# Mamba-2 scan and maxout FFN in one kernel: another order of the first transfers, and the transposes of chunk 2 one step later

## The chip, the cores and the metric

The kernel runs on one core of a Trainium2 chip. The metric is the time of one execution on the device, in microseconds (us); lower is better. A core has a matrix engine (PE, with its weight loads PEld), a vector engine (DVE), a scalar engine (ACT), a general engine (POOL) and a queue engine that issues the transfers (SP, "SPq" in the profile). Each works through its own instructions in the order in which they were written; semaphores tie the engines together. All large transfers of this kernel are issued by SP and go through one queue that feeds sixteen DMA engines.

## The reference

The input is `x` (4 batches, 8 heads, 768 tokens, 32 values), a decay `a` per token, and `B` and `C` (16 values per token and head). Per head it is a gated recurrence over the tokens, here written in pieces of 32 tokens:

```
cum = cumsum(log a)                       # inside the piece
L   = exp(cum_i - cum_j), for j <= i      # decay between two tokens
y   = ((C B^T) * L) x  +  (C state) * exp(cum_i)
state = exp(sum log a) * state + B^T (x * exp(cum_last - cum_j))
```

The eight heads of a token, side by side, are a row of 256 values. All 3072 rows then go through a feed-forward block with a maximum of three products:

```
h   = max(x @ w1, x @ w2, x @ w3)         # 256 -> 768
out = h @ w_out                           # 768 -> 256
```

The activations are float32. The four weight matrices arrive as float64 and are turned into float32 on the chip.

## The kernel before

**Tiling.** The kernel cuts the 768 tokens into six chunks (0 to 5) of 128 tokens, and each chunk of all four batches is a block of 512 rows. For each chunk it computes the scan first, which leaves `yT` (256 x 512), and then the feed-forward block. The decay between tokens needs, for each chunk c, a tile `L` of 128 x 4 x 8 x 128 values: the running sums of log a are stored once to DRAM (`cums`, L713), and each chunk's are loaded back, spread over 128 partitions, in two halves of 1 MB (`decay_load`, L365; pair 0 is batches 0 and 1, pair 2 is batches 2 and 3). `last_load` (L373) loads the same sums in another layout as `E`, in eight small transfers; `load` (L125) loads `B`, `C` and `x` of a chunk. `fetch` (L159) loads one of twelve pieces of the weights, 512 KB each, nine of w1 to w3 and three of w_out. All of these stand in SP's one queue in the order of the program.

**Decoding the weights.** `decode` takes the next fetched piece through ACT (L175, L184), DVE (L176, L179) and POOL (L185); `sign` (L188, DVE) finishes it. This is done once, while chunk 0 is in its feed-forward block.

**The scan of a chunk n.** `transposed(n)` puts `B` and `C` through PE (L403, four transposes each, into `trB` and `trC`), copies `trB` to `BT` on ACT (L399) and, on POOL, makes `Bd` (L434). `scan_c` makes `CT` from `trC` on ACT (L418), `scan_e` is an exponential of `E` on ACT (L422), `scan_cd` multiplies `trC` and `E` on DVE (L429). `decay_masks(n, (b, b'))` masks two batches of `L` on POOL (L377), and `decay_part` takes the exponential of four heads of one batch on ACT (L384). `scores` makes the score products on PE (L474) and leaves their weighting on DVE (L482) for later. `scan_state` is the product for the next state on PE (L444, into a bank called `A`); it returns the rest, `scan_sum`, which is one multiplication on DVE (L455) and two operations on POOL (L460, L463). `scan_old`, `scan_own` make y on PE (L497, L510), `scan_y` copies it to `yT` on ACT (L534), `scan_sums` queues four differences on DVE (L544).

**The feed-forward block.** Chunk 0 is computed by plain products in a loop over n = 0 to 17 (L569), with the decoding and the scan of chunk 1 written between them. Chunks 1 to 5 are computed with seven products of half the size instead of eight, over nine steps k = 0 to 8 (three pairs of columns of each of the three matrices). In a step, `early` issues four products on PE (L619), a copy on ACT (L644) and three additions on DVE (L645 to L647); `late` issues the other three products, which go into the same two PSUM tiles (`sumA` of which there is one, `sumB` of which there are two), and then an operation that empties `sumA` (L658 on ACT, or L660 on DVE) and one that empties `sumB` (L661). The products need sums of weights that POOL makes, four operations for a step (`weight_sums`, L604 to L607); those for steps 2 to 8 are made in chunk 1's block, two steps ahead. `down_next` is a third of a quarter of the product with w_out (L681).

**What sets the order.** The order is written out by hand. While chunk c is in its feed-forward block, the scan of chunk n = c + 1 is written between `early` and `late` of its steps. For c = 1 the tables X1, Y1, P1, D1 and K1 (L855 to L860) say what stands at each step: in X1, "t" is `transposed(n)`, "s0" and "s2" are scores, "A" and "A1" the state product of chunk n and of chunk 1, "y" the end of the scan, "D" a `down_next`. P1 says how many of the operations kept for later (`later`) are taken from the list at three points of a step. The place between chunk 0's last product and chunk 1's step 0 (L842 to L850) is called the seam below.

Of the kernel before, what the change touches and what calls it, by code (L numbers as in the profile page):

```python
# [19 lines left out]
def kernel(  # L20
# [22 lines left out]
    NB, NH, S, D = x.shape  # L43
# [164 lines left out]
    load(0, "C")  # L208
    fetch()
    load(0, "x")  # L210
    for _ in range(4):
        fetch()


    ident = const.tile([P, P], FP32, name="ident")
# [409 lines left out]
    def pop(n):  # L625
        while n and later:
            later.pop(0)()
            n -= 1
# [63 lines left out]
    for b in range(2, NB):  # L692
# [19 lines left out]
    running(R, lg, a_sb)  # L712
    nc.sync.dma_start(  # L713
        out=cums.rearrange("k c s -> (k c) s").rearrange("(w r) s -> r w s", w=2), in_=a_sb)
    decay_load(1, (0,))
    fetch()
    decay_load(1, (2,))
    fetch()
    load(1, "B")
    load(1, "C")  # L720
    fetch()
    last_load(1)
    fetch()
    load(1, "x")
    fetch()
    decode()
    first_exps(2, True, (1,))
    first_exps(3, True, (1,))
# [54 lines left out]
    for n in range(NF * 3):  # L783
        j, g = divmod(n, 2)
        q, i = divmod(j, 3)
        f = 2 * q + g
        if n == 0:
            pair = [ffn_bank([P, BLK], "up") for _ in range(2)]
            for p, ff in zip(pair, range(2)):
                group(p, 0, ff, (0,))  # L790
            first_own((2, 3))
            for p, ff in zip(pair, range(2)):
                group(p, 0, ff, (1,))
        if j > 0:
            p = ffn_bank([P, BLK], "up")
            whole_group(p, i, f)
        else:
            p = pair[g]
        if i == 0 and g == 0:
            m = ffn.tile([P, 4, HB], FP32, tag="m", name="m")  # L800
        if n in (13, 14, 16, 17):
            pop(2)
        mg = m[:, 2 * g:2 * g + 2].rearrange("p r t -> p (r t)")
        if i == 0:
            nc.scalar.copy(out=mg, in_=p)
        else:
            nc.vector.tensor_tensor(
                out=mg if i == 1 else h_of(0)[:, f], in0=mg, in1=p, op=ALU.max)
        if g == 0 and n <= 16:
            sign()  # L810
            if n <= 14:
                decode()
        if n == 1:
            fj = from_last(R, a_sb, "fj")
        if n == 2:
            fetch()
            fetch()
            loads(2)
        if n == 3:
            first_tokens()  # L820
            scan_state(0, att_bank)()
        if n == 4:
            decay_masks(1, (0, 1))
        if n == 9:
            decay_masks(1, (2, 3))
        if n in (5, 7, 9, 11, 13, 14, 15, 16):
            part(1)
        if n == 10:
            transposed(1)
            scan_c(1)  # L830
# [14 lines left out]
    scan_own(1, range(NB))  # L845
    scan_y(1)
    scan_sums(1)
    pop(9)
    transposed(2)
    downs += [(0, j) for j in range(8)]  # L850

    X1 = ["A1", "", "D", "s0", "D", "s2", "A", "y", "D"]  # L855
    Y1 = ["", "", "D", "", "", "D", "D", "D", "D"]
    P1 = [(1, 1, 1), (1, 0, 0), (1, 0, 0), (1, 4, 1), (1, 0, 0), (1, 2, 2), (1, 1, 0), (1, 0, 0),
          (9, 0, 0)]
    D1 = [(1, 0), (1, 0), (2, 0), (1, 0), (2, 0), (1, 0), (0, 2), (0, 1), (0, 2)]
    K1 = {0: (0, (2, 3)), 4: (1, (0, 1)), 6: (1, (2, 3))}  # L860
# [8 lines left out]
    for c in range(1, NC):  # L869
# [4 lines left out]
        for k in range(NW):  # L874
# [79 lines left out]
```

## Time and profile before

| what | value |
|---|---|
| median of 3 runs | 311.21 us (310.51 to 312.63) |
| the profiled execution | 310.39 us, its span 308.7 us |
| mean granted clock of TensorE | 0.983 |
| busy: PE | 284.7 us, 92% of the span |
| busy: DVE, ACT, POOL | 198.6, 120.8 and 72.4 us |
| DMA queue of SP | 104688 packets, 27.66 MB, 44.4% of the 16 engines' span |

All times of the trace count from the start of the span. A row of the timeline names start, length, engine, line, operation, output and inputs, and how many instructions are put together in it; in square brackets stands how long the engine was idle before it and what ended that. A float32 product is shown as two records. A row of a table of windows gives, for one stretch of time, the busy time of each engine, the granted clock of TensorE (1.00 is full speed) and the mean busy share of the DMA engines. A "DMA" piece in the chain of waits reaches from the issue of a transfer to its landing.

### The profile page before, as it was taken

The numbers are of one execution on the slowest core, as the hardware profiler recorded it, in microseconds if no ns is written. First come the engines' busy times: TensorE is split into PE (matmuls) and PEld (weight loads), VectorE is DVE, ScalarE is ACT, GpSimd is POOL, SyncE is SP. The second block draws the span as 40 slices with busy tenths as digits, with TensorE's granted clock in tenths as the row PEclk, the third lists the DMA queues.
The fourth block names the chain that finished last, engine by engine and source line by source line (L and its number), as shares of the span: only waits on it lengthen the run. The fifth ranks groups of instructions, "written<-read, shape, count | busy, mean of one in ns | idle before, by whom it ended". The sixth has DMA issues, their size and how long they took to land.

```text
span 308.7 us, 5285 instructions
## 1 busy us (share of the span) xinstructions
PE 284.7 (92%) x2024; PEld 223.9 (73%) x2024; DVE 198.6 (64%) x382; ACT 120.8 (39%) x313; POOL 72.4 (23%) x96
## 2 busy tenths in 40 slices
PE   6679989718799999999999999999999999999995
PEld 4464344406587888887888888888887888888784
DVE  2757579703787936769577758477767676667530
ACT  2945587405645434524344442535341202011200
POOL 5253663910997150004300006000000000000000
PEclk9999999966999999999999999999999999999999
DMA  7969969989693000988004894001010000010101
GB/s 89 225 237 294 152 181 275 266 92 203 167 113 29 34 2 23 261 114 119 2 0 111 227 110 64 2 4 34 0 36 0 2 0 34 2 35 0 34 2 68
DMA packets 105017, 28.13 MB, mean 91 GB/s; under 512 B 75296, under 2 KB 101920, under 8 KB 104992
## 3 DMA queue, kind: packets, MB, share of 16 engines
q1 hardware_dynamic: 104688, 27.66, 44.4%
q8 instruction: 16, 0.26, 0.4%
q10 hardware_dynamic: 304, 0.13, 0.2%
q14 instruction: 9, 0.07, 0.1%
HBM read 24.54 MB, written 3.24 MB: 90 GB/s over the span
## 4 chain that ended last, share of the span: by engine, by line
PE 68%; DMA 11%; SPq 9%; DVE 5%; ACT 4%; issue 2%; ACTq 0%; DVEq 0%
PE sumB L619 23%; PE o L681 18%; PE sumA L619 18%; SPq L159 5%; DMA L<-cums 4%; SPq L125 3%; PE s L474 2%; PE y L510 2%; DMA rb<-in_moe_w_dram 2%; DMA raw_C<-in_C_dram 2%; DMA cums<-a_sb 2%; DVE L L482 2%; PE y L497 1%; ACT L L384 1%; ACT CT L418 1%
## 5 line engine op out<-in xcount | busy, mean ns | idle before, releaser
L681 PE MATMUL o<-wo,h 128*128 128x256 f32 x288 | 68.8, 379 | 0.0
L681 PEld LDWEIGHTS o<-wo,h 128*128 128x128 f32 x288 | 54.7, 190 | 7.4
L619 PE MATMUL sumA<-yT,w 128*128 128x256 f32 x180 | 56.0, 393 | 1.6 <-DVE m L660 0.9
L384 ACT ACTIVATE L<-L,ncums 128x128 f32<-128x128 f32 x160 | 50.4, 392 | 8.4 <-POOL L L377 8.4
L644 ACT COPY eu<-sumA 128x256 f32<-128x256 f32 x45 | 16.8, 372 | 92.9 <-PE sumA L619 85.4
L619 PE MATMUL sumB<-rb 128*128 128x256 f32 x180 | 47.0, 384 | 0.0
L645 DVE TENSOR_TENSOR eu<-sumA,eu 128x256 f32<-128x256 f32 x45 | 19.0, 422 | 41.6 <-ACT eu L644 41.6
L619 PEld LDWEIGHTS sumA<-yT,w 128*128 128x128 f32 x180 | 32.2, 191 | 10.2 <-issue 2.8
L619 PEld LDWEIGHTS sumB<-rb 128*128 128x128 f32 x180 | 34.8, 193 | 4.9
L569 PE MATMUL up<-yT,w 128*128 128x512 f32 x64 | 29.1, 600 | 1.3 <-DVE w L188 1.3
L482 DVE TENSOR_TENSOR L<-s,L 128x512 f32<-128x512 f32 x46 | 29.2, 679 | 0.4
L619 PE MATMUL sumB<-yT,rb 128*128 128x256 f32 x90 | 27.6, 389 | 1.3 <-DVE rb L647 1.3
L661 DVE TENSOR_TENSOR rb<-sumB,eu 128x512 f32<-128x512 f32 x30 | 20.7, 688 | 10.8 <-PE sumB L619 10.8
L619 PE MATMUL sumA<-rb 128*128 128x256 f32 x90 | 27.2, 385 | 0.0
L619 PE MATMUL sumB<-rb,w 128*128 128x256 f32 x90 | 26.8, 379 | 0.0
L185 POOL TENSOR_TENSOR w_u<-w_u,w_r 128x512 uint32<-128x512 uint32 x12 | 15.3, 1272 | 33.4 <-DVE w_u L179 16.1
L569 PEld LDWEIGHTS up<-yT,w 128*128 128x128 f32 x64 | 11.7, 190 | 15.7 <-issue 10.9
L646 DVE TENSOR_TENSOR v<-sumB,eu 128x256 f32<-128x256 f32 x45 | 19.1, 425 | 5.7 <-PE sumB L619 0.8
L377 POOL TENSOR_SCALAR_AFFINE_SELECT L<-L 128x1024 f32<-128x1024 f32 x20 | 22.3, 1146 | 0.0
L619 PEld LDWEIGHTS sumB<-yT,rb 128*128 128x128 f32 x90 | 16.1, 189 | 6.6 <-DVE rb L647 2.1
L686 ACT COPY ob<-o 128x512 f32<-128x512 f32 x12 | 7.0, 585 | 33.3 <-PE o L681 33.3
L619 PEld LDWEIGHTS sumA<-rb 128*128 128x128 f32 x90 | 17.4, 193 | 2.5
(100 smaller groups left out, 326.3 us busy)
## 6 DMA issues: line engine op xcount, KB each, us to landing
L<-cums SPq DMA_DIRECT2D x10, 1024.0 KB, 9.9
rb<-in_moe_w_dram SPq DMA_DIRECT2D x9, 512.0 KB, 6.8
raw_x<-in_x_dram SPq DMA_DIRECT2D x6, 512.0 KB, 7.4
out_dram<-ob SPq DMA_DIRECT2D x12, 256.0 KB, 2.1
raw_B<-in_B_dram SPq DMA_DIRECT2D x6, 256.0 KB, 4.3
raw_C<-in_C_dram SPq DMA_DIRECT2D x6, 256.0 KB, 6.3
rb<-in_moe_w_out_dram SPq DMA_DIRECT2D x3, 512.0 KB, 6.3
E<-cums SPq DMA_DIRECT2D x40, 32.0 KB, 3.3
```

The costliest lines, as they stand in the source:

```text
L159: nc.sync.dma_start(out=rb.rearrange("p k f w -> p k (f w)"), in_=src)
L185: nc.gpsimd.tensor_tensor(out=u, in0=u, in1=r, op=ALU.add)
L377: nc.gpsimd.affine_select(out=Ls[c][:, b], in_=Ls[c][:, b], pattern=[[0, NH], [1, P]], compare_op=ALU.is_ge, fill=MASKED, base=0, channel_ ...
L384: nc.scalar.activation(L[:, b, h], L[:, b, h], AF.Exp, bias=ncum[c][:, b * NH + h:b * NH + h + 1], scale=1.0)
L482: nc.vector.tensor_tensor(out=M, in0=s, in1=M, op=ALU.mult)
L569: nc.tensor.matmul(out=bank, lhsT=w_sb[i][:, k, f * P:(f + 1) * P], rhs=yT[0][:, k], start=(k == 0), stop=(k == KD - 1))
L619: nc.tensor.matmul(out=bank[:, half], lhsT=left(p, k), rhs=sides[c][p], start=(first and half == 0), stop=True, skip_group_check=True)
L644: nc.scalar.copy(out=eu[:, 0], in_=A[:, 0])
L645: nc.vector.tensor_tensor(out=eu[:, 1], in0=A[:, 1], in1=eu[:, 0], op=ALU.add)
L646: nc.vector.tensor_tensor(out=v, in0=B[:, 1], in1=eu[:, 1], op=ALU.add)
L661: nc.vector.tensor_tensor(out=t[:, 0:2], in0=B, in1=eu[:, 1:2].to_broadcast([P, 2, HB]), op=ALU.add)
L681: nc.tensor.matmul(out=o[:, i], lhsT=hT[c][:, f, b * P:(b + 1) * P], rhs=wo_sb[:, f], start=(f == 0), stop=(f == NF - 1), skip_group_check ...
```

## The change

Three things are changed, and all of them move instructions; none is added or removed.

The first is the order of the transfers. The running sums are stored after three pieces of the weights instead of five. Nine pieces of the weights instead of eight stand ahead of chunk 1's `x`. The transfers of chunk 2 are no longer in the order `L`, `L`, `E`, `B`, `C`, `x` behind all weights, but `B`, `C`, half of `L`, `E`, the other half, `x`, with the last two pieces of the weights between them; and they are written at n = 3 of chunk 0's loop instead of n = 2.

The second is the place of the transposes. Those of chunk 2 move from the seam to step 1 of chunk 1, between `early` and `late`, and `scan_c`, `scan_e` and `scan_cd` of chunk 2 follow them there from step 0. Those of chunk 1 move from n = 10 to n = 11.

The third is the state product of chunk 1, which moves from step 0 to the seam; its rest is taken from the list there.

```diff
@@ the first transfers
     load(0, "x")
-    for _ in range(4):
-        fetch()
+    fetch()
+    fetch()
@@ after the sums are stored
+    fetch()
     decay_load(1, (0,))
     fetch()
     decay_load(1, (2,))
-    fetch()
+    for _ in range(3):
+        fetch()
     load(1, "B")
     load(1, "C")
     fetch()
     last_load(1)
     fetch()
     load(1, "x")
-    fetch()
     decode()
@@ chunk 0's loop
-        if n == 2:
-            fetch()
-            fetch()
-            loads(2)
         if n == 3:
             first_tokens()
             scan_state(0, att_bank)()
+            load(2, "B")
+            fetch()
+            load(2, "C")
+            decay_load(2, (0,))
+            fetch()
+            last_load(2)
+            decay_load(2, (2,))
+            load(2, "x")
...
-        if n == 10:
+        if n == 11:
             transposed(1)
             scan_c(1)
@@ the seam
     scan_sums(1)
+    later.append(scan_state(1, att_bank))
     pop(9)
-    transposed(2)
@@ chunk 1's table
-    X1 = ["A1", "", "D", "s0", "D", "s2", "A", "y", "D"]
+    X1 = ["", "t", "D", "s0", "D", "s2", "A", "y", "D"]
-    P1 = [(1, 1, 1), (1, 0, 0), (1, 0, 0), (1, 4, 1), ...
+    P1 = [(1, 0, 0), (1, 0, 0), (1, 0, 1), (1, 4, 1), ...
@@ the steps
-            elif x == "A1":
-                later.append(scan_state(1, att_bank))
...
             if n < NC and k == 0:
                 loads(c + 2)
+            if x == "t":
                 scan_c(n)
                 scan_e(n)
                 later.append(lambda: scan_cd(n))
```

SP's queue around the store of the running sums, from the weights behind chunk 0's `x` to those ahead of chunk 1's `B`. Before (`rb` is the buffer of a piece of the weights, `a_sb` holds the sums, `L` is chunk 1's):

```order
L159 DMA rb<-in_moe_w_dram 128x2x512 x4
L713 DMA cums<-a_sb 96x2x128
L365 DMA L<-cums 128x16x128
L159 DMA rb<-in_moe_w_dram 128x2x512
L365 DMA L<-cums 128x16x128
```

and now:

```order
L159 DMA rb<-in_moe_w_dram 128x2x512 x2
L713 DMA cums<-a_sb 96x2x128
L159 DMA rb<-in_moe_w_dram 128x2x512
L365 DMA L<-cums 128x16x128
L159 DMA rb<-in_moe_w_dram 128x2x512
L365 DMA L<-cums 128x16x128
L159 DMA rb<-in_moe_w_dram 128x2x512 x3
```

Two pieces of the weights moved behind the store, one of them directly behind it, where it needs no wait for the store.

The same queue from chunk 1's `E` to chunk 2's `x`. Before:

```order
L373 DMA E<-cums 16x4x128 x8
L159 DMA rb<-in_moe_w_dram 128x2x512
L125 DMA raw_x<-in_x_dram 128x32x32
L159 DMA rb<-in_moe_w_out_dram 128x2x512 x3
L365 DMA L<-cums 128x16x128 x2
L373 DMA E<-cums 16x4x128 x8
L125 DMA raw_B<-in_B_dram 128x32x16
L125 DMA raw_C<-in_C_dram 128x32x16
L125 DMA raw_x<-in_x_dram 128x32x32
```

and now:

```order
L373 DMA E<-cums 16x4x128 x8
L159 DMA rb<-in_moe_w_out_dram 128x2x512
L125 DMA raw_x<-in_x_dram 128x32x32
L125 DMA raw_B<-in_B_dram 128x32x16
L159 DMA rb<-in_moe_w_out_dram 128x2x512
L125 DMA raw_C<-in_C_dram 128x32x16
L365 DMA L<-cums 128x16x128
L159 DMA rb<-in_moe_w_out_dram 128x2x512
L373 DMA E<-cums 16x4x128 x8
L365 DMA L<-cums 128x16x128
L125 DMA raw_x<-in_x_dram 128x32x32
```

Chunk 2's `B` and `C` moved from behind its `L` and `E` to ahead of them, and the second half of `L` is now behind `E`.

PE from the last product of chunk 1's scan to step 1. Before (`trB` and `trC` are chunk 2's transposes, `A` is chunk 1's state product; `w_88`, `w_89` are two of the three weight matrices, `rb` sums of weights or of y):

```order
L510 MATMUL y<-L,raw_x 32x128 x32
L403 MATMUL trB<-ident,raw_B 128x128 x4
L403 MATMUL trC<-ident,raw_C 128x128 x4
L619 MATMUL sumA<-yT,w_88 128x256
L619 MATMUL sumA<-rb 128x256
L619 MATMUL sumB<-rb 128x256 x2
L444 MATMUL A<-raw_x,Bd 32x64 x16
L619 MATMUL sumA<-yT,w_88 128x256
L619 MATMUL sumB<-yT,rb 128x256
L619 MATMUL sumB<-rb,w_88 128x256
```

and now, from the row behind `y` to the transposes:

```order
L444 MATMUL A<-raw_x,Bd 32x64 x16
L619 MATMUL sumA<-yT,w_88 128x256
L619 MATMUL sumA<-rb 128x256
L619 MATMUL sumB<-rb 128x256 x2
L619 MATMUL sumA<-yT,w_88 128x256
L619 MATMUL sumB<-yT,rb 128x256
L619 MATMUL sumB<-rb,w_88 128x256
L619 MATMUL sumA<-yT,w_89 128x256
L619 MATMUL sumA<-rb 128x256
L619 MATMUL sumB<-rb 128x256 x2
L403 MATMUL trB<-ident,raw_B 128x128 x4
L403 MATMUL trC<-ident,raw_C 128x128 x4
```

The eight transposes moved behind the seven products of step 0 and the four of step 1's first half, and the state product moved ahead of step 0.

POOL follows: chunk 1's `old` and `S` (L460, L463) now stand ahead of the first decoding at the seam (L185) instead of behind it, and chunk 2's `Bd` (L434) moved from the seam to behind the second masks and the last decoding, ahead of the weight sums of step 3.

More of the change, by code (lines that the diff above doesn't have):

```diff
@@ L847 @@
     scan_sums(1)
+    later.append(scan_state(1, att_bank))
     pop(9)
-    transposed(2)
     downs += [(0, j) for j in range(8)]
-    X1 = ["A1", "", "D", "s0", "D", "s2", "A", "y", "D"]
+    X1 = ["", "t", "D", "s0", "D", "s2", "A", "y", "D"]
     Y1 = ["", "", "D", "", "", "D", "D", "D", "D"]
-    P1 = [(1, 1, 1), (1, 0, 0), (1, 0, 0), (1, 4, 1), (1, 0, 0), (1, 2, 2), (1, 1, 0), (1, 0, 0),
+    P1 = [(1, 0, 0), (1, 0, 0), (1, 0, 1), (1, 4, 1), (1, 0, 0), (1, 2, 2), (1, 1, 0), (1, 0, 0),
           (9, 0, 0)]
```

## The prediction

> **What bounds the kernel now.** I read the page's slices first, to see where the engine that is busy 92% of the span is not.
>
> ```profile
> PE   6679989718799999999999999999999999999995
> PEclk9999999966999999999999999999999999999999
> ```
>
> A slice is 7.7 us. Behind the eleventh, PE stands at 9 to the end, so an earlier start of that stretch is an earlier end of the kernel. The hole is in slices 8 to 10, and there TensorE's clock is low too. The windows cut that place at the edges of the steps of chunk 1: the seam, step 0, step 1, step 2, and steps 3 to 8.
>
> ```profile
> core 0: us, PE busy (x) PEld busy (x) DVE busy (x) ACT busy (x) POOL busy (x), PEclk, DMA share, GB/s
> 60.20:70.90 10.70, 1.75 (x8) 1.41 (x8) 1.51 (x4) 1.48 (x3) 2.54 (x3) 0.69 0.80 108
> 70.90:76.46 5.56, 5.56 (x48) 4.04 (x48) 2.11 (x6) 3.20 (x9) 0.00 (x0) 0.68 1.17 210
> 76.46:82.18 5.72, 3.90 (x16) 2.49 (x14) 4.95 (x11) 4.06 (x10) 5.50 (x8) 1.00 0.88 226
> 82.18:87.90 5.72, 5.72 (x26) 5.05 (x27) 4.55 (x8) 2.71 (x9) 5.64 (x7) 1.00 0.63 85
> 87.90:121.10 33.20, 32.82 (x281) 26.51 (x279) 22.48 (x46) 15.06 (x47) 15.71 (x28) 1.00 0.24 33
> ```
>
> In 10.70 us of the seam PE works 1.75; from step 3 it works 32.82 of 33.20. The granted clock of 0.69 over the seam and 0.68 over step 0 is half speed from 64.3 to 74.5. The chain of waits, asked for the seam, names what ends last:
>
> ```profile
> 49.16 13.85 DMA L<-cums
> 63.02 0.30 SPq L373
> 63.37 0.43 SPq L125
> 63.84 6.25 DMA raw_C<-in_C_dram
> ```
>
> These are transfers, and the queue's order: the second half of chunk 2's `L` lands at 63.0, then come the last `E`, `B`, and `C`, which lands at 70.1. The timeline of PE shows who waits:
>
> ```profile
> 59.77 0.40 PE L510 MATMUL y<-L,raw_x 128*32 128x128 f32 x8
> 67.61 1.08 PE L403 MATMUL trB<-ident,raw_B 128*128 128x128 f32 x4 [7.44 <-DMA raw_B<-in_B_dram]
> 70.23 1.09 PE L403 MATMUL trC<-ident,raw_C 128*128 128x128 f32 x4 [1.53 <-DMA raw_C<-in_C_dram]
> 74.60 0.65 PE L444 MATMUL A<-raw_x,Bd 128*32 128x64 f32 x32
> 79.08 0.70 PE L619 MATMUL sumA<-yT,w 128*128 128x256 f32 x2 [0.52 <-DVE eu L645]
> 80.16 0.67 PE L619 MATMUL sumB<-yT,rb 128*128 128x256 f32 x2 [0.38 <-DVE rb L647]
> 82.18 0.70 PE L619 MATMUL sumA<-yT,w 128*128 128x256 f32 x2 [0.92 <-DVE m L660]
> ```
>
> Step 0 needs none of chunk 2, but stands behind its transposes on PE. In steps 0 and 1 the waits are on DVE.
>
> **The seam without the transposes.** With them gone, PE goes from `y` (ends at 60.2) to the state product, 0.65, and to step 0's first product, if `yT` is there:
>
> ```profile
> 60.02 1.07 ACT L534 COPY yT<-y 128x512 f32<-128x512 f32 x2 [3.50 <-PE y L510]
> 61.84 0.41 DVE L544 TENSOR_TENSOR rb<-y,rb 128x256 f32<-128x256 f32 x1
> 73.47 0.42 DVE L645 TENSOR_TENSOR eu<-sumA,eu 128x256 f32<-128x256 f32 x1 [11.21 <-ACT eu L644]
> 73.33 0.67 ACT L175 ACTIVATE w_u<-rb 128x512 f32<-128x512 f32 x1
> 74.45 1.26 ACT L384 ACTIVATE L<-L,ncums 128x128 f32<-128x128 f32 x4
> 76.18 1.27 ACT L418 ACTIVATE CT<-trC,parity 128x512 f32<-128x512 f32 x2
> 77.33 0.64 ACT L422 ACTIVATE E<-E 128x512 f32<-128x512 f32 x1
> ```
>
> The first copy is there at 60.6, so step 0 starts at 60.85 instead of 70.90: 10.05 us earlier, and PE stands idle for no more than a fraction of a us. Its half clock fell 4.1 us after PE's last product, so I take full speed.
>
> **Step 0.** In step 2, PE is full: 26 records in 5.72 us are 0.22 a record, 0.44 a product, 1.76 for `early`, 1.32 for `late`, 1.32 for a third of a w_out quarter. But at the seam DVE's chain is longer than that. The last difference ends at 62.25, the state's multiplication (the same shape as those of 0.42) at 62.7, and three additions of 0.42, with a little between them, bring it to 64.1; two of `late`'s products follow, so step 0 ends at 65.0. On ACT the copy of the first product (from 61.4), the decoding (twice 0.67) and four exponentials (1.26) end at about 64.4, and the copy that frees `sumA` at 64.8, just in time. Step 0 takes 4.2 instead of 5.56, of which half speed explains most: 1.36 earlier.
>
> **Step 1.** Added are the transposes. What they cost between `early` and `late` is seen in chunk 2, where they stand so already:
>
> ```profile
> 123.00 0.60 PE L403 MATMUL trB<-ident,raw_B 128*128 128x128 f32 x4
> 123.43 0.60 PE L403 MATMUL trC<-ident,raw_C 128*128 128x128 f32 x4
> ```
>
> 0.43 for each four, 0.86 in all. Against that, `CT` (1.27) and `E` (0.64) no longer stand on ACT ahead of step 1's copy, nor `Cd` on DVE ahead of its additions; PE's waits of 0.52 and 0.38 go, and the transposes run in the time of the additions. The wait of 0.92 for L660 stays, since the decoding is still ahead of it. 1.76 + 0.86 + 1.32 + 0.92 = 4.9 instead of 5.72: 0.8 earlier. If none of DVE's waits went, it would be 5.72 + 0.86, 0.9 later; that is the lower end, and I take the upper as nearer, since the rows name the instructions that leave.
>
> **Step 2.** ACT now has the decoding, the exponentials, a copy `BT`, `CT` and `E` between the copies of steps 1 and 2, 5.1 by the rows above with `BT` put at 0.6; the second copy comes at about 71.1, with PE at its `early` from 69.9 to 71.6; a w_out piece (to 72.9) covers the additions. 5.72 stays, and step 3 begins at 75.6 instead of 87.9. The sum so far: 10.05 + 1.36 + 0.8 = 12.2.
>
> **Ahead of the seam.** Two rows show what the store of the sums cost the queue:
>
> ```profile
> 14.99 6.07 DMA cums<-a_sb
> 20.00:22.00 2.00, 1.29 (x31) 0.97 (x22) 0.69 (x1) 0.59 (x1) 0.58 (x1) 1.00 0.02 7
> ```
>
> It landed at 21.06, behind five pieces of the weights, and around that the engines ran empty (busy 0.02). Behind three it lands two pieces earlier, and the piece directly behind it covers most of the hole. That pays for the ninth piece ahead of chunk 1's `x`, so I expect `B`, `C`, `E` and `x` of chunk 1 where they land now. PE's waits in chunk 0 are for decoded weights and not for transfers: I take 0, with 0.5 to either side.
>
> **The queue for chunk 2.**
>
> ```profile
> 42.94 0.47 SPq L125 DMA_DIRECT2D raw_x<-in_x_dram  x1
> 43.45 5.15 SPq L159 DMA_DIRECT2D rb<-in_moe_w_out_dram  x3
> 48.70 5.46 SPq L365 DMA_DIRECT2D L<-cums  x2
> 54.21 9.11 SPq L373 DMA_DIRECT2D E<-cums  x8
> raw_x<-in_x_dram SPq DMA_DIRECT2D x1, 512.0 KB, 7.1
> L<-cums SPq DMA_DIRECT2D x1, 1024.0 KB, 9.3
> ```
>
> The last two rows are the landings of `x` issued at 42.94 (50.0) and of the first half of `L` issued at 48.70 (58.0). From 50.0 to 58.0 the queue moves three weights and a half of `L`, to 63.0 the other half: if that one's 5.0 is the rule, a weight takes 1.0; if the same bytes take the same time, it is 3.2 and 1.6. `E` and `B` take 4.5 more (to the 67.5 at which PE goes on), `C` 2.6; with 2.6 for `B` too, `E` is 1.9. In the new order, from the same 50.0: `B` 52.6, `C` with a weight ahead of it 56.2 to 56.8, the first half of `L` 60.0 to 61.2. The second half has two weights, `B`, `C`, both halves and `E` ahead of its landing: 50.0 + 5.2 + (13.0 less a weight) + 1.9, which is 68.5 to 69.1, with a us to either side for gaps in the queue 67.5 to 70.1. `B` and `C` are called for at 66.8: ten us of slack. `E` is called for on ACT at 70.5. The first half is called for by POOL's masks at the seam and, behind the first mask of 1.2, by ACT's exponentials at about 63: below 61.8 it costs nothing. The second half now lands later than today's 63.0, and POOL stands behind it:
>
> ```profile
> 76.52 1.27 POOL L185 TENSOR_TENSOR w_u<-w_u,w_r 128x512 uint32<-128x512 uint32 x1 [7.81 <-DVE w_u L179]
> 81.48 2.32 POOL L377 TENSOR_SCALAR_AFFINE_SELECT L<-L 128x1024 f32<-128x1024 f32 x2
> 67.62 1.09 POOL L434 TENSOR_TENSOR Bd<-raw_B,from_js 128x512 f32<-128x512 f32 x1 [5.98 <-DMA raw_B<-in_B_dram]
> 87.52 0.45 POOL L607 TENSOR_TENSOR rb<-w,rb 128x128 f32<-128x128 f32 x1
> ```
>
> POOL's line from step 0 is decoding, four sums, masks that wait for this half, decoding, `Bd`, four sums for step 3. Decoding begins at 65.0 (two operations of DVE behind 64.1); with 1.8 for four sums POOL is at the masks at 68.1. Behind them 2.32 + 1.27 + 1.09 and 1.4 for three of the four sums are 6.1, and step 3's second product calls for the third at 76.0. So up to 69.9 the half of `L` costs nothing, and behind that each us costs one. Its range gives 0 to 0.2; since POOL was full in steps 1 and 2 (5.50 and 5.64 of 5.72) and leaves nothing over, I put 0.2.
>
> [...]
>
> **The sum.** 12.2 - 0.2 = 12.0 us off the profiled execution's 310.39 (of which 308.7 is span and 1.7 lies around it): 298.4. The median of the runs is 311.21, 0.8 above that execution, so I put 298.6. Behind step 3 nothing is changed but that chunk 3's transfers follow `x` of chunk 2 about two us earlier.
>
> **Rivals.** *The masks' half of L comes late.* POOL waits, and step 3 with it. At 73.0 (another 3 us, as by a gap like the one at the store) it costs 3.1, and the time is 301.7. For it: it stands at the end of a line of fourteen transfers, and its landing took 13.85. Against it: the range above is made of the same transfers. Chance 0.15.
>
> *The wait only moves.* If the new order brought nothing and `C` landed at 70.1 as today, PE would stand from 66.8 to 70.2 in step 1, and the gain would be 12.0 - 3.4 = 8.6, and the time 302. Against it: `C` then followed three weights, `L` and `E`, and now a single weight and `B`. Chance 0.04. Here the clock has a say: half speed came 4.1 us behind PE's last product and lasted 10.2, so a wait of 3.4 would just not bring it. [...]
>
> *Slower.* The same line of POOL, far enough: decoding stands behind the masks, and so do all weight sums from step 3 on. If the second half of `L` landed beyond 82 the gain would be gone, and beyond 85 the kernel slower by over 1%, about 314. In the trace a half never took more than 13.85 from its issue, and it would have to be issued at 71. Chance 0.02.
>
> **How the numbers follow.** The forecast has 0.79, with 297.1 to 300.3 for its own range: 0.2 for `L`, 0.5 ahead of the seam and 0.8 between the execution and the median to the one side, 1.7 for step 1's lower end to the other. The range goes 0.3 below that and reaches to the first two rivals: 296.8 to 302. One per cent, about what a measurement of this kernel can tell from no change, is 3.1 us; all cases but the last and a worse form of it are faster by more. Faster 0.95, same 0.03, slower 0.02.
>
> **What would show it.** PE's row before `sumA` of step 0 without a wait for a transfer, and the granted clock at 1.00 in all windows; step 0's first product near 60.9 and step 3's near 75.6; the transposes in step 1 with no wait. POOL's masks behind `ws` of step 2 waiting for `L` under 1.5 us. I am wrong if PE waits in step 1 for `raw_C`, if step 3 waits for POOL, or if chunk 0 ends later than 60.7.

## The result and the profile after

The changed kernel takes 301.27 us, the median of 4 runs (300.64 to 303.39), beside 311.67 us for the kernel before on the same chip (310.51 to 312.63). The ratio is 0.968, with a 95% interval of 0.962 to 0.974: 3.2% faster. In a later comparison it was 300.86 us and 0.970 (0.965 to 0.975). Medians and ratios leave out two slow runs, one of that comparison (304.99 us) and one of the run "copy beside a product" below (319.42 us). The profiled execution took 300.64 us, of which 298.8 is span.

The page's slices of the kernel after, PE's busy tenths and TensorE's clock:

```profile
PE   6769989978999999999999999999999999999994
PEclk9999999999999999999999999999999999999998
```

The 7, 1 and 8 of slices 8 to 10 have become 9, 7 and 8, and the two 6 of the clock are gone.

The windows of the kernel after, cut at the same edges as before: from the end of chunk 1's `y` to step 0's first product, step 0, step 1, step 2, and steps 3 to 8.

```profile
core 0: us, PE busy (x) PEld busy (x) DVE busy (x) ACT busy (x) POOL busy (x), PEclk, DMA share, GB/s
60.58:61.06 0.48, 0.44 (x32) 0.28 (x21) 0.02 (x1) 0.48 (x2) 0.00 (x0) 1.00 1.05 382
61.06:66.30 5.24, 3.77 (x15) 2.60 (x16) 4.15 (x10) 3.37 (x9) 3.45 (x4) 1.00 0.40 119
66.30:71.22 4.92, 4.13 (x24) 3.21 (x22) 4.17 (x10) 3.86 (x10) 3.37 (x5) 1.00 1.09 257
71.22:77.72 6.50, 6.15 (x26) 4.77 (x26) 4.90 (x8) 3.71 (x11) 6.49 (x7) 1.00 1.24 205
77.72:111.30 33.58, 33.24 (x282) 26.92 (x283) 23.73 (x47) 15.21 (x48) 16.56 (x29) 1.00 0.49 80
```

The seam shrank from 10.70 us to 0.48. Step 0 took 5.24 (forecast 4.2), step 1 took 4.92 (4.9), step 2 took 6.50 (5.72). Step 3 begins at 77.72 instead of 87.90, and from there to the end it is 298.8 - 77.72 = 221.1 us, against 308.7 - 87.90 = 220.8 before. So all of the gain lies ahead of step 3, and 10.2 us of the forecast's 12.2 are there.

The timeline of the kernel after, rows of step 0:

```profile
61.06 0.70 PE L619 MATMUL sumA<-yT,w 128*128 128x256 f32 x2
62.14 0.67 PE L619 MATMUL sumA<-rb 128*128 128x256 f32 x2 [0.38 <-DVE rb L544]
62.85 0.37 ACT L644 COPY eu<-sumA 128x256 f32<-128x256 f32 x1 [1.35 <-PE sumA L619]
63.25 0.42 DVE L645 TENSOR_TENSOR eu<-sumA,eu 128x256 f32<-128x256 f32 x1 [0.27 <-ACT eu L644]
63.70 0.59 PE L619 MATMUL sumB<-rb 128*128 128x256 f32 x2 [0.46 <-DVE eu L645]
64.79 0.42 DVE L647 TENSOR_TENSOR m<-sumB,v 128x256 f32<-128x256 f32 x1
65.36 0.67 PE L619 MATMUL sumB<-yT,rb 128*128 128x256 f32 x2 [0.64 <-DVE m L647]
```

DVE's chain sets step 0, as forecast, but it starts later: the copy runs at 62.85 and not at 61.4, behind the second product into `sumA`, which itself had waited 0.38 for a difference on DVE, and the fourth product comes 0.46 late. L647 ends at 65.21 instead of the forecast's 64.1. And rows of step 2 of the same timeline:

```profile
64.92 0.43 SPq L365 DMA_DIRECT2D L<-cums  x1
71.22 0.70 PE L619 MATMUL sumA<-yT,w 128*128 128x256 f32 x2 [0.79 <-DVE m L660]
71.23 2.13 POOL L377 TENSOR_SCALAR_AFFINE_SELECT L<-L 128x1024 f32<-128x1024 f32 x2 [1.15 <-DMA L<-cums]
73.33 1.27 POOL L185 TENSOR_TENSOR w_u<-w_u,w_r 128x512 uint32<-128x512 uint32 x1
74.64 1.57 DVE L188 SCALAR_TENSOR_TENSOR wo<-rb,w_u 128x512 uint32<-128x512 uint32 x1 [0.44 <-POOL w_u L185]
76.26 0.73 PEld L681 LDWEIGHTS o<-wo,h 128*128 128x128 f32 x4 [0.43 <-DVE wo L188]
77.72 0.48 PE L619 MATMUL sumA<-yT,w 128*128 128x256 f32 x1 [0.33 <-DVE h L660]
```

The second half of chunk 2's `L` was issued at 64.92 and landed at 71.17, later than the 67.5 to 70.1 of the forecast. POOL waited for it, the last decoding stood behind the masks, the last `sign` (L188) behind the decoding, and the w_out product of step 2 behind that. The wait of rival 1 is there, 1.15 us of it, and PE pays for it in step 2, ahead of where I had looked for it. The landing is not the whole of it: L188 took 1.57 here, beside POOL's `Bd`, and 0.68 in step 1. With 0.68 it would have ended at 75.32 by these rows (an estimate), ahead of the 75.83 at which PE was ready for it. No run moves `Bd`, so what the late landing would cost without that is not shown.

### The profile page after: what moved, and what is told of

Read it like the earlier page. It is cut to its first block, busy times and chain, and to the rows that moved or that the text cites. A ratio compares the mean times of both kernels' runs of the same rounds, so it can differ in the third digit from the quotient of the medians.

```text
span 298.8 us, 5292 instructions
## 1 busy us (share of the span) xinstructions
PE 282.9 (95%) x2024; PEld 222.6 (74%) x2024; DVE 199.7 (67%) x382; ACT 120.7 (40%) x313; POOL 72.2 (24%) x96
## 4 chain that ended last, share of the span: by engine, by line
PE 79%; DVE 6%; issue 4%; DMA 3%; ACT 3%; POOL 2%; SPq 2%; POOLq 0%; DVEq 0%; ACTq 0%
PE sumB L619 23%; PE o L681 19%; PE sumA L619 17%; PE up L569 7%; PE s L474 3%; PE y L510 3%; DMA raw_x<-in_x_dram 3%; PE y L497 2%; DVE L L482 2%; PE up L561 1%; ACT L L384 1%; SPq L125 1%; POOL w_u L185 1%; DVE v L646 1%; SPq L159 1%
## 5 line engine op out<-in xcount | busy, mean ns | idle before, releaser
L681 PE MATMUL o<-wo,h 128*128 128x256 f32 x288 | 69.1, 379 | 0.0
L619 PE MATMUL sumA<-yT,w 128*128 128x256 f32 x180 | 55.4, 390 | 1.3 <-DVE m L660 0.8
L619 PE MATMUL sumB<-rb 128*128 128x256 f32 x180 | 46.4, 379 | 0.5 <-DVE eu L645 0.5
L645 DVE TENSOR_TENSOR eu<-sumA,eu 128x256 f32<-128x256 f32 x45 | 19.0, 423 | 30.7 <-ACT eu L644 30.7
L619 PEld LDWEIGHTS sumB<-rb 128*128 128x128 f32 x180 | 34.2, 190 | 5.3 <-issue 0.6
L569 PEld LDWEIGHTS up<-yT,w 128*128 128x128 f32 x64 | 11.7, 190 | 15.7 <-issue 10.9
L185 POOL TENSOR_TENSOR w_u<-w_u,w_r 128x512 uint32<-128x512 uint32 x12 | 15.2, 1270 | 27.0 <-DVE w_u L179 9.2
```

Source lines behind the costliest of these rows:

```text
L185: nc.gpsimd.tensor_tensor(out=u, in0=u, in1=r, op=ALU.add)
L569: nc.tensor.matmul(out=bank, lhsT=w_sb[i][:, k, f * P:(f + 1) * P], rhs=yT[0][:, k], start=(k == 0), stop=(k == KD - 1))
L619: nc.tensor.matmul(out=bank[:, half], lhsT=left(p, k), rhs=sides[c][p], start=(first and half == 0), stop=True, skip_group_check=True)
L645: nc.vector.tensor_tensor(out=eu[:, 1], in0=A[:, 1], in1=eu[:, 0], op=ALU.add)
L681: nc.tensor.matmul(out=o[:, i], lhsT=hT[c][:, f, b * P:(b + 1) * P], rhs=wo_sb[:, f], start=(f == 0), stop=(f == NF - 1), skip_group_check ...
```

## Experiments

The edits are diffs to the kernel before (for the two halves of the change) or to the changed kernel (for all others). The traces reach step 0 of chunk 1 up to 3 us apart, two of the same kernel 0.9 apart, so I compare the steps from step 0's first product on. The two traces of "masks later", which get there last, have a stretch of half speed in chunk 0 (18.01 to 21.42 and 16.60 to 23.43), which no other of these traces has. For the kernel before, the steps are counted from the first products at 71.11 and 76.67; the 70.90 and 76.46 of the windows ahead of the change are the starts of their weight loads. All steps in us:

| kernel | first product | step 0 | step 1 | step 2 | first product to step 3 | median (runs) | ratio to before |
|---|---|---|---|---|---|---|---|
| before | 71.11 | 5.56 | 5.51 | 5.72 | 16.79 | 311.67 (4) | 1 |
| after | 61.06 | 5.24 | 4.92 | 6.50 | 16.66 | 301.27 (4) | 0.968 (0.962 to 0.974) |
| after, again | 61.92 | 5.83 | 5.50 | 5.72 | 17.05 | 300.86 (5) | 0.970 (0.965 to 0.975) |
| moves alone | 61.54 | 4.76 | 6.49 | 5.72 | 16.97 | 302.25 (4) | 0.970 (0.966 to 0.974) |
| transfers alone | 62.36 | 4.41 | 6.48 | 7.40 | 18.29 | 303.25 (4) | 0.972 (0.968 to 0.976) |
| `L` ahead of `E` | 61.46 | 4.96 | 5.69 | 5.72 | 16.37 | 301.31 (4) | 0.970 (0.964 to 0.976) |
| `L` behind `x` | 61.74 | 4.79 | 5.02 | 9.42 | 19.23 | 303.94 (4) | 0.976 (0.973 to 0.979) |
| copy beside a product | 60.59 | 4.41 | 5.32 | 6.07 | 15.80 | 313.56 (5) | 1.012 (1.007 to 1.017) |
| masks later | 62.85 | 4.77 | 4.76 | 5.72 | 15.25 | 300.34 (6) | 0.969 (0.965 to 0.972) |
| masks later, again | 63.82 | 4.77 | 4.76 | 5.72 | 15.25 | 299.44 (7) | 0.961 (0.957 to 0.964) |
| both | 61.36 | 5.84 | 5.47 | 6.08 | 17.39 | 315.37 (6) | 1.016 (1.013 to 1.020) |
| order in step 0 alone | 61.61 | 4.75 | 5.06 | 5.72 | 15.53 | 301.14 (6) | 0.967 (0.962 to 0.971) |

The first four experiments shared one set of runs of before (median 311.48, 7 runs), the next four another (310.23, 11 runs, "after, again" among these), and "masks later, again" and the last a third (311.40, 11 runs).

### The moves alone

The kernel before, with chunk 2's transposes and the state product moved and the transfers as they were. Chunk 1's transposes stay at n = 10, here and in the next run.

```diff
+    later.append(scan_state(1, att_bank))
     pop(9)
-    transposed(2)
...
-    X1 = ["A1", "", "D", "s0", "D", "s2", "A", "y", "D"]
+    X1 = ["", "t", "D", "s0", "D", "s2", "A", "y", "D"]
...
```

> The instructions are moved (chunk 2's transposes to step 1, chunk 1's state product to the seam), the transfers stay in the order of before. Theory: either half of the change takes away most of the wait. Chunk 2's C still lands near 70.1, so PE waits in step 1, from about 68.0 to 70.2; but the second half of L lands at 63.0, so step 2 takes 5.7 instead of the 6.5 of the changed kernel. Step 3 begins near 79, and the time is about 302.3, within 1% of the changed kernel. Rival, the order of the transfers carries the gain: with it undone, more than half of the 10 us is lost and the time is above 306.

It took 302.25 us. PE's waits in these steps, from the trace's view of waits (what waited, for what, in total, times, longest):

```profile
PE trC L403 <- DMA raw_C<-in_C_dram: 1.7, 1, 1.7
PE sumA L619 <- DVE m L660: 0.4, 1, 0.4
```

`C` lands late as it did before, and PE now has steps 0 and half of step 1 to do until then: the 10 us at the seam become a wait of 1.70. Rival 2 priced just this case at 302. Its price came out, its wait did not: PE reached the transposes of `C` at 68.7 and not 66.8, since step 0 began 0.7 later and took 0.6 longer than I had put, and the transposes of `B`, 0.6, come first.

### The transfers alone

The kernel before with the new order of transfers; the transposes stay at the seam.

```diff
...
-        if n == 2:
-            fetch()
-            fetch()
-            loads(2)
...
         if n == 3:
             first_tokens()
             scan_state(0, att_bank)()
+            load(2, "B")
+            fetch()
+            load(2, "C")
+            decay_load(2, (0,))
+            fetch()
+            last_load(2)
+            decay_load(2, (2,))
+            load(2, "x")
```

> The transfers go in the new order, the instructions stay where they were (chunk 2's transposes at the seam, chunk 1's state product in step 0). Theory: C is there at 56.7, so the transposes at the seam cost 0.9 and no wait, the clock stays at full speed, and the second half of L is as late as in the changed kernel (71.2). Step 0 begins near 61.9, step 3 near 79.5, and the time is about 303. Rival, the moves carry the gain: above 306.

It took 303.25 us. The transposes ran at the seam with no wait (61.43 to 62.36), and with that wait went the half speed at the seam. What was lost again shows in the timeline of this run ahead of step 2's first product:

```profile
71.31 2.50 POOL L377 TENSOR_SCALAR_AFFINE_SELECT L<-L 128x1024 f32<-128x1024 f32 x2
71.67 1.19 DVE L179 TENSOR_SCALAR w_u<-w_u 128x512 uint32<-128x512 uint32 x1
73.25 0.91 PE L619 MATMUL sumA<-yT,w 128*128 128x256 f32 x2 [1.56 <-DVE m L660]
```

DVE's second pass over the weights, 0.43 elsewhere, takes 1.19 beside POOL's masks; PE waits 1.56 for what stands behind it. I had put the time at about 303, but without a loss in the clock and with step 3 near 79.5; it began at 80.65. The product pair of 0.70 takes 0.91: the clock fell to half speed at 73.61, for 3.41 us (last section), which made step 2 7.40. So either half of the change takes away 8 to 9 of the 10 us by itself, because both remove the same wait, PE standing at the seam for chunk 2's `B` and `C`. Behind the moves, the order of the transfers is worth 1.0 us by the medians, whose intervals overlap, and 0.3 in the traces. In the executions whose granted clock was 0.997 or more, the moves alone took 301.18 and 301.31 us (two of four), the transfers alone 300.96 (one of four) and both together 300.64, 301.08 and 301.46 (three of four). So what either half adds to the other is not shown.

### `L` ahead of `E`

The changed kernel, with the second half of `L` issued ahead of the eight transfers of `E`.

```diff
-            last_load(2)
             decay_load(2, (2,))
+            last_load(2)
             load(2, "x")
```

> The changed kernel with the second half of chunk 2's L ahead of its E instead of behind. Theory: step 2's 6.5 us (0.8 over the forecast) come from POOL, which waits for that half until 71.2. It now lands at 67 to 68, POOL's masks start without a wait, step 2 takes 5.7, and the time is 0.8 us below the changed kernel's, about 300.4. Rival, the 0.8 us come from ACT and DVE, which have the transposes' copies and the decoding in front of them: step 2 stays at 6.5 and the time at 301.2.

It took 301.31 us, no different from the changed kernel. But the trace shows two effects of opposite sign. The half landed at 68.38 instead of 71.17, POOL's masks found it, and step 2 fell back to 5.72. Step 1 grew from 4.92 to 5.69. The timeline of this run:

```profile
70.17 2.50 POOL L377 TENSOR_SCALAR_AFFINE_SELECT L<-L 128x1024 f32<-128x1024 f32 x2
70.53 1.20 DVE L179 TENSOR_SCALAR w_u<-w_u 128x512 uint32<-128x512 uint32 x1
72.11 0.70 PE L619 MATMUL sumA<-yT,w 128*128 128x256 f32 x2 [1.56 <-DVE m L660]
```

In the changed kernel L179 took 0.43 with the masks a little behind it; here the masks are under way when it starts, and it takes 1.20. L660 and step 2 wait for it. The masks themselves take 2.50 instead of 2.13.

### `L` behind `x`

The other direction: the half is moved behind chunk 2's `x`.

```diff
             last_load(2)
-            decay_load(2, (2,))
             load(2, "x")
+            decay_load(2, (2,))
```

> The changed kernel with the second half of chunk 2's L behind its x. Theory: POOL's line has no slack left, so the half lands about 4 us later (near 75) and the start of step 3 moves with it, one for one: about 305. Rival, there is slack behind POOL's masks: less than 1.5 us are lost, under 302.8.

It took 303.94 us. The half landed at 74.44, 3.27 later than in the changed kernel. POOL's row and PE's in step 2:

```profile
74.50 2.14 POOL L377 TENSOR_SCALAR_AFFINE_SELECT L<-L 128x1024 f32<-128x1024 f32 x2 [4.08 <-DMA L<-cums]
79.52 1.52 PE L681 MATMUL o<-wo,h 128*128 128x256 f32 x4 [2.95 <-DVE wo L188]
```

Step 2 grew by 2.92, from 6.50 to 9.42, and step 3 began 3.25 later, at 80.97 instead of 77.72. So past the point where POOL begins to wait, the landing counts one for one in these two traces, as rival 1 had it, and the place is the w_out product of step 2. The median grew by 2.67, less than the 4 or so that I had put.

### The copy beside a product

The changed kernel, with the four products of `early` in another order in every step, and ScalarE's copy behind the second of them.

```diff
-        products(c, k, [(1, A, 0), (6, A, 1), (5, B, 0), (7, B, 1)], True)
+        products(c, k, [(1, A, 0), (5, B, 0)], True)
+        eu = wtmp.tile([P, 2, HB], FP32, tag="w_u", name="eu")
+        nc.scalar.copy(out=eu[:, 0], in_=A[:, 0])
+        products(c, k, [(6, A, 1), (7, B, 1)], True)
...
-        nc.scalar.copy(out=eu[:, 0], in_=A[:, 0])
```

> After, with one order of four products changed in every step: first, third, second, fourth (the two into sumA are no longer neighbours), and ScalarE's copy of the first issued behind the third, so that it waits for the first alone and runs beside the third. Theory (step 0 took 5.24 instead of 4.2 because the copy waits for both products into sumA and VectorE's chain of three sums hangs on it): the copy starts 0.8 us behind step 0's first product instead of 1.8, step 0 takes 4.3 to 4.6 and step 1 some 4.5; but the second half of the decays still lands near 71.2, so that step 2 grows by what steps 0 and 1 lose, and step 3 begins 16.3 to 16.6 behind step 0's first product (16.66 after): time 301.0. Rival (the fourth product's wait on TensorE, or the hand-over between engines, sets step 0, and the second product now waits for the copy in every step): step 0 stays at 5.1 or more and the time is 302 or more.

It took 313.56 us, 1.2% slower than the kernel before. In step 0 the theory held: the copy ran 0.74 behind the first product, and step 0 took 4.41. Step 1 then took 5.32, where I had put 4.5, and from step 3 on the loss adds up. The group rows for the weight loads of the second product into `sumA`, first of the changed kernel:

```profile
L619 PEld LDWEIGHTS sumA<-rb 128*128 128x128 f32 x90 | 17.0, 190 | 3.1 <-issue 0.8
```

then of this run:

```profile
L619 PEld LDWEIGHTS sumA<-rb 128*128 128x128 f32 x90 | 13.4, 188 | 21.5 <-ACT eu L637 16.9 <-issue 2.4 <-POOL rb L607 1.1
```

The copy stands ahead of that product in the program, and by the second row the product's loads waited for it, 16.9 us in sum over 45 steps. In step 0 this costs nothing, since PE waits for DVE's chain there anyway; where PE is full it is paid. From step 3 to the end this run took 310.5 - 76.39 = 234.1 us instead of 221.1: 13.0 more, less the 1.3 us by which step 3 began earlier (76.39 and 77.72), which is the 11.7 between the two spans; the medians of this comparison lie 12.7 apart. My rival named the mechanism but set its price no higher than 302 or more.

### The masks later

The run with `L` ahead of `E`, and POOL's masks of that half moved from behind step 0's weight sums to behind step 1's.

```diff
-    K1 = {0: (0, (2, 3)), 4: (1, (0, 1)), 6: (1, (2, 3))}
+    K1 = {1: (0, (2, 3)), 4: (1, (0, 1)), 6: (1, (2, 3))}
```

> The earlier run with the second half of the decays ahead of the last decays, and GpSimd's masks of that half moved behind the weight sums of step 1, out of the time of VectorE's two passes over the weights. Theory (in that run step 1 lost 0.77 us because VectorE's second pass, 1.20 us instead of 0.43, stood beside the masks): second pass back to 0.43 to 0.7, step 1 4.9 and step 2 5.7, step 3 15.6 to 15.9 behind step 0's first product (16.37 in that run, 16.66 after); time 300.3 to 300.6. Rival (the masks only collide with something else, or the exponentials of step 3 now wait for them): 16.3 or more, time 301.2.

It took 300.34 us, and 299.44 in a second comparison. Its timeline shows L179 free of the masks:

```profile
71.57 0.43 DVE L179 TENSOR_SCALAR w_u<-w_u 128x512 uint32<-128x512 uint32 x1
72.14 1.27 POOL L185 TENSOR_TENSOR w_u<-w_u,w_r 128x512 uint32<-128x512 uint32 x1 [1.71 <-DVE w_u L179]
72.38 0.70 PE L619 MATMUL sumA<-yT,w 128*128 128x256 f32 x2 [0.53 <-DVE m L660]
```

Step 1 took 4.76, step 2 took 5.72, and step 3 begins 15.25 behind step 0's first product, in both traces: 1.4 less than in the changed kernel's shorter trace, 1.8 less than in the other. Of the 1.4, 0.5 lie in step 0, where only the late fourth product is missing; against the run with `L` ahead of `E`, step 1 gained 0.93. The theory holds for the steps. In time it is not shown against the changed kernel: in the same comparison the difference is 0.5 us (300.34 and 300.86), within the intervals of the two ratios, and the second comparison did not hold the changed kernel. That 299.44 is below the 300.0 to 300.8 I had put.

### The changed kernel again

> The changed kernel once more, beside the three before, for differences below one per cent: 301.0 to 301.6, step 3 16.4 to 17.0 behind step 0's first product.

It took 300.86 us; step 3 began 17.05 behind step 0's first product. Both are just outside what I had put. The 16.66 and 17.05 have different parts, with the same program:

```profile
65.15 0.59 PE L619 MATMUL sumB<-rb 128*128 128x256 f32 x2 [1.05 <-DVE eu L645]
71.50 2.32 POOL L377 TENSOR_SCALAR_AFFINE_SELECT L<-L 128x1024 f32<-128x1024 f32 x2 [0.84 <-DMA L<-cums]
71.60 1.27 DVE L179 TENSOR_SCALAR w_u<-w_u 128x512 uint32<-128x512 uint32 x1
```

Here the fourth product of step 0 waited 1.05 instead of 0.46. That pushed DVE's second pass into the masks, and it took 1.27 instead of 0.43: step 1 went from 4.92 to 5.50, and step 2, no longer short of its weights, back to 5.72.

### Both, and the order in step 0 alone

The edits of the two runs "copy beside a product" and "masks later" together, with the state's multiplication and sums taken from the list in step 0 instead of at the seam:

```diff
-    pop(9)
+    pop(4)
     downs += [(0, j) for j in range(8)]
```

> The edits of the two runs before this one together, and the state's two sums taken out of VectorE's queue between the differences and step 0's first sum. Theory: step 0 4.3 to 4.5, step 1 4.5, step 2 5.7: step 3 14.6 to 14.9 behind step 0's first product; time 299.2 to 299.6. Rival (GpSimd's chain of sums, masks and weight sums, about 13 us of it in these three steps, becomes the bound): 15.6 or more, time 300.3 or more.

It took 315.37 us. From step 3 to the end it took 313.1 - 78.75 = 234.4 us, as the run above with that order in every step, and step 0's fourth product waited 1.26. Neither the theory nor the rival had foreseen that, since the cost of that order was not yet known when this run was planned. Then the same with the new order in step 0 of chunk 1 alone:

```diff
...
+        if c == 1 and k == 0:
+            products(c, k, [(1, A, 0), (5, B, 0)], True)
+            nc.scalar.copy(out=eu[:, 0], in_=A[:, 0])
+            products(c, k, [(6, A, 1), (7, B, 1)], True)
+        else:
+            products(c, k, [(1, A, 0), (6, A, 1), (5, B, 0), (7, B, 1)], True)
+            nc.scalar.copy(out=eu[:, 0], in_=A[:, 0])
```

> The run with the masks later, and the other order of four products in step 0 of the second chunk alone (first, third, second, fourth, with ScalarE's copy behind the third), the state's two sums behind step 0's first three sums. Theory (what was lost in the run that had the order in every step is TensorE's wait for the copy, 0.45 us a step from step 1 on, and step 0 itself gains): step 0 4.2 to 4.5 and steps 1 and 2 as with the masks later (4.76 and 5.72): step 3 14.7 to 15.0 behind step 0's first product, time 299.6 to 300.1. [...]

> The run with the masks later once more, beside the last: 300.0 to 300.8, step 3 15.2 to 15.7 behind step 0's first product.

It took 301.14 us, where I had put 299.6 to 300.1, and 15.53 to step 3, 0.28 longer than with the masks later alone. That the order in every step was what made the two runs slow is confirmed. That step 0 then gains is not: it took 4.75, with the fourth product at 63.66, 0.17 behind the end of the third. Step 1 took 5.06 instead of 4.76: POOL's two sums of the state came in it, ahead of the weight sums, and these now stood beside DVE's passes:

```profile
69.25 0.91 POOL L605 TENSOR_TENSOR rb<-w 128x128 f32<-128x128 f32 x1
69.77 0.67 DVE L176 TENSOR_SCALAR w_u<-w_u 128x512 f32<-128x512 f32 x1
70.48 0.56 DVE L179 TENSOR_SCALAR w_u<-w_u 128x512 uint32<-128x512 uint32 x1
```

In the run with the masks later, they took 0.46, 0.42 and 0.43. Whether the order gains anything in step 0 without that late product, this run can't say; the run with the order in every step, where no product was late, had 4.41.

## Why the prediction was right, and where it was wrong

**What bounded the kernel** was read rightly: PE waited at the seam for chunk 2's `B` and `C`. Either half of the change by itself brings 8 to 9 us; both together bring 10.4, by the medians.

**The seam.** Step 0's first product was forecast at 60.85 and came at 61.06, in a trace whose `y` ended at 60.58, 0.4 later than before. The granted clock was 1.00 in all five windows, as forecast.

**Step 0** was mis-sized: 4.2, measured 5.24. The step that failed is "on ACT the copy of the first product from 61.4". The copy waits for both products into `sumA`, not for the first, and came 1.8 behind the first product's start. Of the 1.04 us, 0.46 is the late fourth product; without it step 0 takes 4.76 to 4.77 ("moves alone", "masks later"), 0.57 over the forecast. With the copy freed of its second product it took 4.41; of the 0.2 that is left, the two products behind the additions make most, 1.09 to step 1 instead of 0.9.

**Step 1** came out: 4.92 for 4.9, the transposes without a wait, and the wait for L660 0.79 where I had kept 0.92. It held by luck of timing: in the second trace of the same kernel DVE's pass met the masks and the step took 5.50.

**The queue.** `B` was forecast at 52.6 and landed at 52.85, `C` at 56.2 to 56.8 and 56.71, the first half of `L` at 60.0 to 61.2 and 61.75, 0.55 past its range and just inside the 61.8 up to which it costs nothing. The second half, forecast at 68.5 to 69.1 with 67.5 to 70.1 as bounds, landed at 71.17. This is the step that failed. My sum started from chunk 1's `x` at 50.0, which came at 50.88 although the store of the sums had landed at 18.74 instead of 21.06; and it took the queue to be full all the time. SP's waits in the kernel after, between 50 and 70:

```profile
SPq L373 <- DMA rb<-in_moe_w_out_dram: 2.5, 1, 2.5
SPq L373 <- DMA L<-cums: 1.0, 1, 1.0
```

and the window around the issue of the half, of the same kernel:

```profile
64.00:65.00 1.00, 0.72 (x4) 0.29 (x2) 0.64 (x2) 1.00 (x4) 0.94 (x2) 1.00 0.05 14
```

SP stood at the last of `E`'s eight small transfers until the piece of the weights issued eight transfers earlier had landed (64.56), while the DMA engines ran empty at 0.05, and only then could the half be issued. Nothing in a transfer of `E` needs the weights. With the half issued ahead of `E` it landed at 68.38. That is 2.8 earlier, but by my sum, without the 1.9 of `E`, it would have been 66.6 to 67.2, so SP's wait is not all that the sum had wrong, and the rest stays open. The same wait is in the rows of before that I quoted and misread: `L` landed at 63.02 and the last `E` was issued at 63.02, and not by the queue's order alone: SP held that `E`, with `B` and `C` behind it, for 0.6 us until `L` was there.

**Step 2 and rival 1.** "Up to 69.9 the half of `L` costs nothing, and behind that each us costs one": 71.17 is 1.27 past it, and step 2 cost 0.78 more. With the half at 74.44, it was 2.92 more than that for 3.27. The slope is right and the free time was half a us longer than I put. One reason is that POOL itself came to the masks at 70.08 and not at 68.1, since the decoding ahead of them began at 66.64 and not at 65.0; so the landing cost POOL only 1.15. The place was wrong: not step 3's weight sums but the last decoded piece of w_out, which step 2 multiplies by. I had looked for who waits for POOL among its own results and not behind DVE's `sign`. My sign of being wrong, "if step 3 waits for POOL", came true one step early.

**Rival 2** was right in its price by accident (302, "moves alone" 302.25), and wrong in what it says of the clock: a wait of 3.4 us "would just not bring it". In the run with `L` behind `x`, a wait of 2.95 us was followed by half speed (from 80.12 to 83.53, below).

**The sum.** Step 3 was forecast at 75.67 (75.6 in the text) and came at 77.72: 0.21 late at the seam, 1.04 in step 0, 0.02 in step 1, 0.78 in step 2, which is 2.05. Less the 0.2 already allowed for `L`, and with 0.28 more behind step 3 and 0.15 more outside the span, 298.4 becomes 300.7; the profiled execution took 300.64. The median of 301.27 is outside the 297.1 to 300.3 of the forecast's own case and inside the range, which had been drawn to 302 for the rivals, and one of them is part of what happened. The forecast of the median, 298.6, was also added up wrongly: it lay 0.2 above the execution's 298.4, where the rows before had shown 0.8. It is 0.63 above it here.

## What to carry to other kernels

Where a wait is removed that one engine had for one transfer, ask first whether the edits that remove it are alternatives: here two of them, each by itself, brought 8 to 9 of 10 us, and the next waits set the rest. Before adding up a queue from its bytes, look at what its issuing engine waits for: in this program a transfer that needs nothing was still held until one issued eight places earlier had landed, so eight small transfers ahead of a large one that was urgent cost SP a wait of 2.5 us at the last of them. And a move that takes work off a wait puts it beside something else; on POOL and DVE that alone cost 0.8 us, and an order of products that gained 0.4 us in one step lost 13 in the others, where its wait had no cover.

## What the runs showed of the hardware

**DVE and POOL took longer beside each other.** DVE's pass L179 took 0.43 with POOL waiting and 1.19 to 1.27 where POOL's masks were under way when it started; the masks took 2.32 to 2.50 there instead of 2.13. DVE's `sign` L188 took 0.68 in step 1 of the kernel after and 1.57 beside POOL's `Bd` in step 2. With the masks elsewhere ("masks later"), L179 is at 0.43 again. With `L` ahead of `E`, L179 started at 70.53, within the first of two masks that had begun at 70.17 and took 2.50 together, so that the first ended near 71.4 (an estimate: half of the 2.50); L179 ended at 71.73, some 0.3 behind that. What held it in between, no row tells.

**Half speed lasted 3.41 us or a multiple of it, and came not only behind an idle PE.** The windows of the run with the transfers alone, the last 3.41 us at full speed and the next 3.41:

```profile
70.20:73.61 3.41, 1.47 (x7) 1.01 (x7) 3.38 (x6) 0.75 (x3) 3.33 (x4) 1.00 1.06 111
73.61:77.02 3.41, 3.41 (x10) 2.66 (x9) 0.88 (x3) 1.98 (x7) 3.33 (x7) 0.50 1.08 283
```

and of the run with `L` behind `x`:

```profile
76.71:80.12 3.41, 0.60 (x3) 0.55 (x4) 2.22 (x2) 0.00 (x0) 3.41 (x4) 1.00 1.21 290
80.12:83.53 3.41, 3.41 (x9) 2.30 (x8) 2.00 (x4) 0.40 (x2) 3.25 (x7) 0.50 0.53 121
```

In both runs the 3.41 us at half speed came behind 3.41 us in which PE was busy for 1.47 and for 0.60. In the kernel before, half speed lasted 10.24, three times that, and in the 3.41 us ahead of it PE did nothing (60.82 to 64.23); in the kernel after, the record of full speed lasts from 7.03 to 297.16, which is 85 times that. Counted in the same steps from the clock's changes, these are a window of the kernel before and one of "masks later" with what came behind it:

```profile
13.03:16.44 3.41, 1.61 (x43) 1.15 (x39) 3.38 (x7) 3.34 (x7) 2.56 (x3) 1.00 1.00 311
14.60:18.01 3.41, 1.57 (x36) 0.97 (x32) 3.41 (x6) 2.69 (x6) 3.39 (x3) 1.00 1.05 388
18.01:21.42 3.41, 2.97 (x7) 2.43 (x8) 1.80 (x5) 1.53 (x3) 2.06 (x2) 0.50 0.48 151
```

Behind the 1.61 (47% of the 3.41) the clock stayed at 1.00, behind the 1.57 (46%) it fell. Whether PE's busy time is what counts is not shown. Half speed for 3.41 us cost PE up to 1.7 us of work (an estimate: half of the 3.41), and in the run with the transfers alone PE's longest wait ahead of it was 1.56.

**SP waited for the transfer eight places ahead.** In the kernel after, `E`'s seventh was issued at 61.77 when the half of `L` eight places ahead had landed at 61.75, and the eighth at 64.57 when the weights eight places ahead had landed at 64.56. In that trace the landings of SP's transfers are recorded on eight semaphores in turn, and each of these two shares one with the transfer that it waited for.

**A late product, and a transfer ahead of it.** The fourth product of step 0 waited in five of the ten traces below, 0.46 and 1.05 in two of the same program, and no instruction of the kernel explains it: the profile names DVE's L645 for the wait, but with `L` ahead of `E` the product started at 63.83 and L645 ended at 64.08. The trace also records the transfers of the queue named "instruction" on the page, 16 of 16 KB each. The start and end of the third of them, and the start of that product with its wait:

```
kernel                    starts   ends    product starts (its wait)
after                     61.26    62.30   63.70 (0.46)
after, again              62.48    63.64   65.15 (1.05)
both                      62.15    63.08   64.50 (1.26)
order in step 0 alone     61.33    62.29   63.66 (0.17)
L ahead of E              61.61    62.57   63.83 (0.18)
masks later               62.32    63.38   64.87 (no wait)
masks later, again        63.28    64.42   65.83 (no wait)
L behind x                61.06    62.06   63.76 (no wait)
copy beside a product     59.66    60.62   62.31 (no wait)
moves alone               59.11    60.26   63.56 (no wait)
```

The product starts 1.3 to 1.5 us behind the end of that transfer wherever it waits, and nowhere earlier than that. In the kernel before and with the transfers alone, the product stands at another place among PE's instructions, ahead of the state product, so they are left out. No run moved this transfer, nor does the trace say whose instructions it holds, so what the product waited for is not shown.
